# A pooled attention and gMLP kernel: the same instructions issued in another order

## The chip, the cores and the metric

The kernel runs on one core of a Trainium2 chip. The metric is the device time of one execution in microseconds (us). A core has four engines that compute, each with a queue of its own that is worked off in order: TensorE (PE in the profile; its weight loads are listed apart as PEld), VectorE (DVE), ScalarE (ACT) and GpSimd (POOL). SyncE (SP) issues all DMA transfers of this kernel, also in order.

## The reference

```python
# q, k, v: 8 batches x 8 heads x 576 rows x 64
k_p = k.reshape(B, H, 72, 8, D).mean(axis=3)          # pooled by 8
v_p = v.reshape(B, H, 72, 8, D).mean(axis=3)
scores = scale * np.matmul(q, k_p.transpose(0, 1, 3, 2))
attn = softmax(scores)                                 # over the 72 pooled keys
x = np.matmul(attn, v_p)                               # -> 8 x 576 x 512, heads side by side
h = gelu(x @ w_in)                                     # 512 -> 1024
u, v = h[..., :512], h[..., 512:]
v_n = (v - mean(v)) / sqrt(var(v) + 1e-6) * g_ln       # along the 512
v_s = einsum('ts,bsd->btd', w_sg, v_n) + b_sg          # mixes the 576 rows
out = x + (u * v_s) @ w_out
```

All is float32. The kernel reaches that precision on PE by splitting an operand into a high part and a rest (names that end in `hi`/`lo` or `h`/`l`) and adding three products.

## The kernel before, in words

The work on a batch is cut into steps, each a Python generator; one call of `next` records the step's next piece, up to its next `yield`. A step's name is a letter and a number: tile 2 of step H is H2.

- A, B: load k and v, each in two halves (`kvraw`). C: load q of two heads (`qraw`). E: load the last 8 pooled rows of k and v (`left`).
- K: pool k and make the block-diagonal weights `kbd`; for batch 0 the pooling is done by 8 accumulating matmuls with the identity, for the others by a reduction on DVE. K2 reduces `left` into `lp`, transposes it on PE (L317) and writes `kbd`. P: the same for v; for batch 0, P2 leaves the masked v rows in the `left` tile itself.
- Q: transpose q on DVE (L372, `qT`). S: scores of two heads on PE, their maximum on DVE (`nmax`, L389), ten exponentials on ACT (`e`, L406), one over the sum on POOL and DVE (L412 to L417), copies of the last columns on POOL (`el`).
- L and T: transpose `el` and `e` on PE (L126), copy on ACT to `lt` and `ah`. V: attention times v, then `x` and its split `xhl`.
- H: x times the v half of w_in, Gelu (`vg`, L510 to L516), normalisation, split to `vhh`, `vhl`. U: x times the u half, Gelu (`u`, L553). W: row mixing with w_sg, then `u` times it (L567, L569) and the split `ghi`, `glo`. O: times w_out, plus x. Z: transpose on DVE and store.
- In small letters stand the weights, once: `lv`, `lu`, `lo`, `ls` load them, v, u, o convert a chunk of w_in or w_out (ACT L186, DVE L190 to L192, ACT L194 and L195, POOL L197 to L199), s transposes and splits a piece of w_sg (PE L221, ACT L147 or L227, DVE L149).

Two tables of such names set the order. `PROLOGUE` is run once; it holds the weights, batch 0 up to its middle, and the start of batches 1 and 2. `PERIOD` is then run for each batch: `H1+0` is the next piece of H1 of this batch, `T0+1` one of the next batch, `Z1-1` one of the batch before. The order in the table is the order in each engine's queue, because every instruction is tied to the one before it on its engine:

```python
    emit(PROLOGUE, 0)
    for b in range(1, B + 3):
        emit(PERIOD, b)
    assert all(next(x, "done") == "done" for x in going.values())
    last = {}
    for ins in nc.cur_bb.bb.instructions:
        if ins.engine in last:
            tc.add_manual_dep(ins, last[ins.engine], mybir.DependencyInfo(
                mybir.DependencyClass.NoSync, mybir.DependencyReason.DATA), reason="order of issue")
        last[ins.engine] = ins.name
```

All matmuls are recorded by the helper `mm` (L92). PSUM has two rings of two tiles each: `mps` (scores of batch 0, weight chunks of the v half, s, H, U, W, O) and `aps` (scores of the other batches, pooling, T, L, V). A ring's tile can only be written anew when its last reader has gone.

Of the kernel before, what the change touches and what calls it, by code (L numbers as in the profile page):

```python
# [20 lines left out]


PROLOGUE = """
lv0 A1+0 K1+0 A0+0 v0 K1+0 K0+0 C0+0 E0+0 v0 Q0+0 C1+0 K2+0 K0+0 v1 v0 v1 K2+0 lv1 C2+0 K2+0 B0+0 Q1+0 S0+0 S0+0
S1+0 S0+0 S1+0 S0+0 A0+1 S1+0 Q2+0 S2+0 C3+0 S0+0 T0+0 v1 P0+0 v0 v1 S2+0 S1+0 T0+0 Q3+0 B1+0 ls0 S2+0 lu0 S3+0
S3+0 P1+0 S2+0 S3+0 S3+0 lo0 S2+0 v2 S3+0 S1+0 A1+1 C0+1 P2+0 v2 v2 v3 s3 L0+0 T1+0 v3 s3 v2 K0+1 L0+0 V0+0 v3
T1+0 V0+0 lu1 v3 u0 u0 u1 u1 V1+0 V1+0 s3 T2+0 T2+0 T3+0 u0 Q0+1 s1 K1+1 u1 V2+0 C1+1 T3+0 u0 V3+0 u2 u2 V0+0 s1
E0+1 s1 V3+0 s2 V2+0 s4 s2 Q1+1 s4 K2+1 V3+0 K2+1 u1 K2+1 S0+1 V3+0 S1+1 V1+0 V2+0 u2 B1+1 s2 P1+1 u3 S0+1 s4
V0+0 C2+1 V1+0 H1+0 S0+1 H0+0 u3 H1+0 B0+1 u2 s0 P0+1 u3 P2+1 u3 C3+1 S0+1 S0+1 Q3+1 A1+2 S1+1 Q2+1 S2+1 s0 o0
H1+0 H0+0 S1+1 s0 S2+1 H0+0 C0+2 K1+2 S1+1 U2+0 A0+2 S2+1 H1+0 H1+0 U2+0 H3+0 H0+0 o0 H1+0 H0+0 S3+1 V2+0 H4+0  # L30
S2+1 T0+1 Q0+2 o0 H0+0 H3+0 S3+1 H4+0 P2+1 o0 S3+1 H3+0 H2+0 H4+0 H2+0 K0+2 S3+1 H3+0 H4+0 U0+0 S2+1 U3+0 S3+1
U0+0 T0+1 S1+1 H3+0 L0+1 P2+1 H4+0 H2+0 H2+0 U1+0 H3+0 H2+0 T0+1 P2+1 L0+1 T1+1 L0+1 L0+1 U3+0 H4+0 C2+2 H2+0
V0+1 o1 lo1 o1 T1+1 B0+2 H4+0 H4+0 W0+0 E0+2 o1 T1+1 K2+2 o1 V1+1 U1+0 V0+1 o2 W1+0 K2+2 W0+0 o2 V1+1 T2+1 B1+2
W2+0 o2 T2+1 o3 o3 K2+2 o3 T2+1 C1+2 V2+1 o2 W2+0 T3+1 V2+1 W1+0 S0+2 o3 W3+0 S0+2 T3+1 W1+0 W2+0 W2+0 Q1+2 W0+0
W0+0 W1+0 S0+2 T3+1 W3+0 V3+1 O1+0 V3+1 P1+2 W3+0 O0+0 Q2+2 S0+2 P0+2 S1+2 S1+2 W3+0 V1+1 O1+0 C3+2 A1+3 S0+2
O1+0 S2+2 O0+0 V2+1 V0+1 V3+1 P2+2 Z1+0 O2+0 O0+0 C0+3 S1+2 O2+0 S2+2 S1+2 O2+0 Z0+0 Z0+0 H2+1 S2+2 V3+1 T0+2
H2+1 A0+3 V1+1 Q3+2
""".split()
PERIOD = """
H1+0 H1+0 P2+1 U3+0 T0+1 Z1-1 H2+0 H2+0 H2+0 H1+0 C1+2 S2+1 H1+0 P2+1 S3+1 O3-1 H2+0 V2+0 S3+1 O3-1 H1+0 Z2-1  # L40
K1+2 U3+0 H1+0 S1+1 V0+0 S3+1 H3+0 O3-1 K0+2 H3+0 H0+0 H0+0 S3+1 H4+0 S3+1 T0+1 B0+2 H4+0 H3+0 H3+0 H3+0 H0+0
H4+0 S2+1 Q1+2 U2+0 H0+0 H3+0 U1+0 H4+0 Z2-1 H4+0 H0+0 L0+1 U2+0 P2+1 H0+0 H4+0 U0+0 L0+1 L0+1 H4+0 L0+1 V0+1
T1+1 U1+0 Z3-1 H4+0 U0+0 E0+2 W0+0 T1+1 V0+1 T1+1 V1+1 W0+0 Q0+2 V1+1 T2+1 T2+1 W2+0 T2+1 C3+2 W2+0 T3+1 W0+0
V2+1 T3+1 V2+1 T3+1 K2+2 W1+0 B1+2 W2+0 K2+2 W0+0 W1+0 V3+1 V2+1 V1+1 K2+2 W1+0 V3+1 W3+0 P1+2 W1+0 W3+0 Z3-1
W2+0 S0+2 S1+2 O0+0 V3+1 S0+2 O1+0 C2+2 A1+3 S1+2 W3+0 Q2+2 P0+2 W3+0 O0+0 S0+2 S0+2 O1+0 S2+2 V0+1 O0+0 Z0+0
V3+1 S2+2 H2+1 S1+2 V1+1 P2+2 O1+0 Z1+0 Q3+2 S2+2 Z0+0 H2+1 S1+2 O2+0 S0+2 O2+0 T0+2 A0+3 C0+3 O2+0
""".split()


# [619 lines left out]
```

## Time and profile before

| | |
|---|---|
| runs shown | 611.53, 609.78, 611.51 us; median 611.51 |
| the profiled execution's own time | 601.74 us, span 600.0 us |
| mean granted clock of TensorE | 0.975 |
| busy: PE, DVE, ACT, POOL | 93%, 67%, 61%, 40% |
| chain that ended last | PE 83%, ACT 6%, DVE 3%, POOL 3%, DMA 2% |

The profile is that of one further execution; all places below are in microseconds from the start of its span. A row of the timeline has the start, the duration, the engine, the line of the program, the operation, what is written and read, how many instructions are merged into it, and in brackets how long the engine stood idle before it and for whom. A row of the waits has who waited for whom, the total, how often and the longest. A matmul of float32 operands leaves more than one record. The granted clock is 1.00 or 0.50 of TensorE's full rate at any moment.

### The profile page before, as it was taken

The page shows a single profiled execution, that of the slowest core. Times are in us where ns is not written, and L with a number is a line of the kernel's source. Part 1 is how long each engine was busy: PE and PEld are TensorE (multiplying, and loading weights), DVE is VectorE, ACT ScalarE, POOL GpSimd, SP SyncE. Part 2 cuts the span into 40 slices and gives each one's busy share as a digit, 9 for nine tenths or more (in the row PEclk, how much of TensorE's full clock was granted, in tenths as well). Part 3 has the DMA queues.
Part 4 walks back from the last instruction along what each step waited for, and adds up shares of the span by engine and source line. Part 5 has one row for each costly group of instructions (what it writes and reads, how often), then busy time and mean ns, then how long its engine had stood idle before and what let it go on. Part 6 is the DMA issues. An engine that isn't in the chain of part 4 may idle for free.

```text
span 600.0 us, 10376 instructions
## 1 busy us (share of the span) xinstructions
PE 559.0 (93%) x3769; PEld 523.1 (87%) x3769; DVE 401.1 (67%) x532; ACT 363.4 (61%) x1093; POOL 239.6 (40%) x336
## 2 busy tenths in 40 slices
PE   4568589999999999999999999999999999999995
PEld 3454468899899998999899999999899989998995
DVE  2566689778866777587856786677857765434444
ACT  1687599786864775567754974577654885312310
POOL 2276486466333534053425333253315233343230
PEclk9779698999999999999999999999999999999998
DMA  7994624313542253515341334416250210021104
GB/s 195 240 271 103 160 55 126 73 21 74 114 93 37 51 99 66 104 36 100 70 93 28 87 58 92 76 36 116 56 103 11 39 21 14 8 36 25 21 1 79
DMA packets 165954, 46.33 MB, mean 77 GB/s; under 512 B 153424, under 2 KB 153424, under 8 KB 165904
## 3 DMA queue, kind: packets, MB, share of 16 engines
q1 hardware_dynamic: 165904, 45.69, 35.7%
q8 instruction: 29, 0.48, 0.3%
q14 instruction: 21, 0.17, 0.1%
HBM read 36.23 MB, written 9.44 MB: 76 GB/s over the span
## 4 chain that ended last, share of the span: by engine, by line
PE 83%; ACT 6%; DVE 3%; POOL 3%; DMA 2%; SPq 1%; issue 1%; DVEq 0%; ACTq 0%; POOLq 0%
PE mps L92 68%; PE aps L92 12%; PE aps L126 3%; ACT e L406 3%; DMA left<-in_v 1%; SPq L144 1%; DMA raw<-in_moe_w_in 1%; DVE lp L294 1%; POOL wil L199 1%; POOL vg L197 1%; POOL top L198 1%; ACT L406 0%; DVE x L594 0%; PE mps L221 0%; ACT ah L449 0%
## 5 line engine op out<-in xcount | busy, mean ns | idle before, releaser
L578 POOL TENSOR_TENSOR glo<-u,ghi 128x576 fp32r<-128x576 f32 x32 | 45.3, 1429 | 112.7 <-ACT ghi L576 112.7
L92 PE MATMUL mps<-xhl,wih 128*128 128x288 f32 x512 | 89.8, 297 | 0.0
L406 ACT ACTIVATE e<-aps,nmax 128x72 f32<-128x72 f32 x280 | 85.4, 350 | 2.1 <-DVE nmax L389 1.8
L92 PE MATMUL mps<-wih,xhl 128*128 128x512 f32 x256 | 86.2, 403 | 0.1
L92 PEld LDWEIGHTS mps<-xhl,wih 128*128 128x128 f32 x512 | 75.8, 188 | 1.6 <-ACT vg L516 0.2
L406 ACT ACTIVATION_READ_ACCUMULATOR e<-aps,nmax 128x1 f32 x280 | 66.0, 236 | 0.0
L567 DVE SCALAR_TENSOR_TENSOR mps<-mps,gcol,bbc 128x576 f32<-128x576 f32 x32 | 26.4, 825 | 53.0 <-PE mps L92 53.0
L92 PEld LDWEIGHTS mps<-wih,xhl 128*128 128x128 f32 x256 | 48.6, 190 | 10.8 <-DVE x L594 0.3
L92 PE MATMUL mps<-wsh,vhh 128*128 128x288 f32 x256 | 55.9, 300 | 0.0
L92 PE MATMUL mps<-ghi,woh 128*128 128x288 f32 x256 | 55.9, 299 | 0.1
L92 PE MATMUL mps<-xhl,wil 128*128 128x288 f32 x256 | 55.0, 296 | 0.0
L92 PE MATMUL mps<-glo,woh 128*128 128x288 f32 x256 | 54.9, 296 | 0.0
L92 PE MATMUL mps<-wsh,vhl 128*128 128x288 f32 x256 | 54.8, 295 | 0.0
L92 PE MATMUL mps<-wsl,vhh 128*128 128x288 f32 x256 | 54.8, 295 | 0.0
L92 PE MATMUL mps<-ghi,wol 128*128 128x288 f32 x256 | 54.7, 294 | 0.0
L483 POOL TENSOR_TENSOR xhl<-x,xhl 128x576 fp32r<-128x576 f32 x32 | 45.2, 1424 | 23.2 <-ACT xhl L481 23.2
L526 DVE TENSOR_SCALAR vg<-vg,mv,rstd 128x512 f32<-128x512 f32 (+1 forms) x40 | 39.4, 987 | 20.2 <-POOL rstd L524 20.1
L92 PE MATMUL mps<-wil,xhl 128*128 128x512 f32 x128 | 50.8, 397 | 0.0
L516 ACT ACTIVATE vg<-mps 128x512 f32<-128x512 f32 x32 | 19.1, 598 | 46.0 <-PE mps L92 45.8
L536 POOL TENSOR_TENSOR vhl<-vg,vhh 128x512 fp32r<-128x512 f32 x32 | 42.1, 1317 | 9.9 <-ACT vhh L534 9.9
L412 POOL TENSOR_TENSOR ssum<-ssum,eps 128x10 f32<-128x10 f32 x32 | 7.0, 217 | 97.2 <-ACT e L406 97.1
L576 ACT CAST ghi<-u 128x576 fp32r<-128x576 f32 x32 | 21.3, 673 | 37.6 <-DVE u L569 37.6
(137 smaller groups left out, 1431.0 us busy)
## 6 DMA issues: line engine op xcount, KB each, us to landing
qraw<-in_q SPq DMA_DIRECT2D x128, 72.0 KB
out<-y SPq DMA_DIRECT2D x128, 72.0 KB
kvraw<-in_k SPq DMA_DIRECT2D x32, 256.0 KB
kvraw<-in_v SPq DMA_DIRECT2D x32, 256.0 KB
raw<-in_moe_w_in SPq DMA_DIRECT2D x4, 1024.0 KB
raw<-in_moe_w_out SPq DMA_DIRECT2D x2, 1024.0 KB
stage<-in_moe_w_sg SPq DMA_DIRECT2D x4, 288.0 KB
left<-in_k SPq DMA_DIRECT2D x16, 64.0 KB
```

What stands on the lines that cost most here:

```text
L92: nc.tensor.matmul(o, lhsT, rhs, start=start, stop=stop)
L126: nc.tensor.transpose(ps[:rows, i * P:(i + 1) * P], src(i), ident if i < NT - 1 else swap)
L144: nc.sync.dma_start(o, i)
L406: nc.scalar.activation(e[:, i, h], slots[i][:, h], AF.Exp, bias=nmax[:, i, h:h + 1], **acc)
L412: nc.gpsimd.tensor_tensor(ssum, ssum, eps[:, 0:1].unsqueeze(2).broadcast_to([P, NT, 2]), op=ALU.add)
L483: nc.gpsimd.tensor_tensor(xhl[:, 1, g], x32[:, g], xhl[:, 0, g].bitcast(F32), op=ALU.subtract)
L516: nc.scalar.activation(vg, o, AF.Gelu_apprx_tanh)
L526: nc.vector.tensor_scalar(vg, vg, mv[:, 0:1], rstd, op0=ALU.subtract, op1=ALU.mult)
L536: (nc.gpsimd if i < NT - 1 else nc.vector).tensor_tensor(lo, vg, hi.bitcast(F32), op=ALU.subtract)
L567: nc.vector.scalar_tensor_tensor(vs, vs, gcol[:, d:d + 1], bbc.rearrange("p (a n) -> p a n", a=2), op0=ALU.mult, op1=ALU.add)
L576: nc.scalar.copy(ghi[:, d], uf)
L578: nc.gpsimd.tensor_tensor(glo[:, d], uf, ghi[:, d].bitcast(F32), op=ALU.subtract)
```

## The change

The two tables have other contents. No step, tile or instruction is added or taken away, only their order differs, in every queue. The first line of each table:

```diff
 PROLOGUE = """
-lv0 A1+0 K1+0 A0+0 v0 K1+0 K0+0 C0+0 E0+0 v0 Q0+0 C1+0 K2+0 K0+0 v1 v0 v1 K2+0 lv1 C2+0 K2+0 B0+0 Q1+0 S0+0 S0+0
+A0+0 lv0 E0+0 A1+0 v1 K0+0 v0 C1+0 K2+0 v1 K0+0 Q1+0 C0+0 K1+0 K1+0 v0 Q0+0 K2+0 K2+0 v1 S0+0 B0+0 v0 C3+0 v1
...
 PERIOD = """
-H1+0 H1+0 P2+1 U3+0 T0+1 Z1-1 H2+0 H2+0 H2+0 H1+0 C1+2 S2+1 H1+0 P2+1 S3+1 O3-1 H2+0 V2+0 S3+1 O3-1 H1+0 Z2-1
+T0+1 H2+0 H1+0 V2+0 Z2-1 V0+0 H1+0 H2+0 S2+1 H4+0 H2+0 H4+0 U3+0 S3+1 Z1-1 P2+1 H4+0 H1+0 O3-1 O3-1 H4+0 H1+0
```

Three places of the beginning, first as they stood and then as they stand.

SP's queue at the very start. Before:

```order
L144 DMA raw<-in_moe_w_in 128x2x1024
L144 DMA kvraw<-in_k 64x2x512 x4
L144 DMA qraw<-in_q 32x18x32 x4
L144 DMA left<-in_k 32x1x512 x2
L144 DMA left<-in_v 32x1x512 x2
L144 DMA qraw<-in_q 32x18x32 x4
```

And after the change:

```order
L144 DMA kvraw<-in_k 64x2x512 x2
L144 DMA raw<-in_moe_w_in 128x2x1024
L144 DMA left<-in_k 32x1x512 x2
L144 DMA left<-in_v 32x1x512 x2
L144 DMA kvraw<-in_k 64x2x512 x2
L144 DMA qraw<-in_q 32x18x32 x8
L144 DMA kvraw_187<-in_v 64x2x512 x2
```

The first half of k moves to the front, `left` ahead of the second half and of all q tiles.

PE's queue from the first scores of batch 0 to its first V (`ah,vb`), before:

```order
L92 MATMUL mps<-kbd,qT 128x144 x15
L126 MATMUL aps<-ident,e 128x128 x4
L126 MATMUL aps<-swap,e 128x128
L92 MATMUL aps<-kvraw_186,ident 128x128 x8
L92 MATMUL mps<-kbd,qT 128x144 x5
L92 MATMUL aps<-kvraw_186,ident 128x128 x8
L221 MATMUL mps<-ident,stage 128x128 x4
L221 MATMUL mps<-ident,stage 128x64
L126 MATMUL aps<-ident,el 64x128 x4
L126 MATMUL aps<-swap,el 64x128
L126 MATMUL aps<-ident,e 128x128 x4
L126 MATMUL aps<-swap,e 128x128
```

After:

```order
L92 MATMUL mps<-kbd,qT 128x144 x10
L92 MATMUL aps<-kvraw_187,ident 128x128 x8
L92 MATMUL mps<-kbd,qT 128x144 x5
L126 MATMUL aps<-ident,e 128x128 x4
L126 MATMUL aps<-swap,e 128x128
L92 MATMUL mps<-kbd,qT 128x144 x5
L92 MATMUL aps<-kvraw_187,ident 128x128 x8
L126 MATMUL aps<-ident,el 64x128 x4
L126 MATMUL aps<-swap,el 64x128
L126 MATMUL aps<-ident,e 128x128 x4
L126 MATMUL aps<-swap,e 128x128
L221 MATMUL mps<-ident,stage 128x128 x4
```

The first pooling of v (P0, `kvraw` with `ident`) moves ahead of the third scores, and the first transposes of w_sg (`stage`) move behind L0 (`el`) and T1 (`e`).

ACT's queue from the softmax of S0 of batch 1, before:

```order
L406 ACTIVATE e,ssum<-aps,nmax 128x72 x10
L516 ACT_TABLE_LOAD
L516 ACTIVATE vg<-mps 128x512
L194 ACTIVATE raw<-raw 128x4x128
L195 CAST wih<-top 128x4x128
L351 ACTIVATE vbh<-vp 64x4x64 x2
L147 CAST wsh<-mps 128x576
L186 ACTIVATE top<-raw 128x512
L516 ACTIVATE vg<-mps 128x512
L406 ACT_TABLE_LOAD
L406 ACTIVATE e,ssum<-aps,nmax 128x72 x20
L534 CAST vhh<-vg 128x512
```

After:

```order
L406 ACTIVATE e,ssum<-aps,nmax 128x72 x10
L516 ACT_TABLE_LOAD
L516 ACTIVATE vg<-mps 128x512
L351 ACTIVATE vbh<-vp 64x4x64 x2
L516 ACTIVATE vg<-mps 128x512
L406 ACT_TABLE_LOAD
L406 ACTIVATE e,ssum<-aps,nmax 128x72 x10
L147 CAST wsh<-mps 128x576
L406 ACTIVATE e,ssum<-aps,nmax 128x72 x10
L516 ACT_TABLE_LOAD
L516 ACTIVATE vg<-mps 128x512
L534 CAST vhh<-vg 128x512 x2
```

The weight pieces (L194, L195, L186) leave this place, ahead of the softmax or behind it, the w_sg copy (L147) moves between the softmaxes of S1 and S2, and the Gelu of a third H comes at once behind them.

More of the change, by code (lines that the diff above doesn't have):

```diff
@@ L23 @@
 PROLOGUE = """
-lv0 A1+0 K1+0 A0+0 v0 K1+0 K0+0 C0+0 E0+0 v0 Q0+0 C1+0 K2+0 K0+0 v1 v0 v1 K2+0 lv1 C2+0 K2+0 B0+0 Q1+0 S0+0 S0+0
[L25 to L37, printed above, removed]
+A0+0 lv0 E0+0 A1+0 v1 K0+0 v0 C1+0 K2+0 v1 K0+0 Q1+0 C0+0 K1+0 K1+0 v0 Q0+0 K2+0 K2+0 v1 S0+0 B0+0 v0 C3+0 v1
+S0+0 A0+1 S0+0 S1+0 S1+0 P0+0 C2+0 S0+0 Q2+0 S1+0 S1+0 S2+0 Q3+0 v0 T0+0 T0+0 S1+0 lv1 S2+0 S0+0 S2+0 B1+0 S3+0
@@ new lines @@
+S3+0 S3+0 C0+1 P1+0 Q0+1 S2+0 S2+0 ls0 P2+0 v2 lu0 S3+0 v2 S3+0 v2 C1+1 v3 L0+0 v2 T1+0 L0+0 v3 v3 K0+1 s1 V0+0
+v3 lo0 Q1+1 T1+0 V0+0 T2+0 u0 A1+1 V1+0 T2+0 s1 s1 V1+0 T3+0 lu1 s3 V0+0 u1 u0 u1 s3 u0 V2+0 s3 K1+1 T3+0 u1
+V2+0 V3+0 V0+0 V1+0 s2 s2 s2 E0+1 u0 B1+1 K2+1 u2 K2+1 u1 u2 C2+1 V3+0 K2+1 s4 B0+1 u2 u3 P1+1 S0+1 u3 S0+1 V2+0
+V3+0 s4 V1+0 S1+1 u2 s4 H0+0 P0+1 H1+0 Q2+1 u3 S0+1 S1+1 H0+0 S0+1 P2+1 S2+1 s0 H1+0 A1+2 u3 S1+1 C3+1 H1+0 s0
+Q3+1 S2+1 H2+0 H0+0 S2+1 S0+1 C0+2 S1+1 s0 H2+0 H1+0 H1+0 S1+1 P2+1 S3+1 S2+1 H1+0 H0+0 H2+0 H0+0 H0+0 H3+0 U3+0
@@ new lines @@
+V3+0 V2+0 T0+1 lo1 o0 S3+1 H2+0 P2+1 P2+1 H3+0 S2+1 U3+0 H2+0 H2+0 H3+0 H3+0 H4+0 U1+0 C1+2 S3+1 o0 H4+0 S3+1
+H4+0 T0+1 o0 S3+1 T0+1 K1+2 L0+1 A0+2 H3+0 H4+0 U0+0 o0 U1+0 U2+0 L0+1 H3+0 T1+1 H4+0 L0+1 o2 L0+1 U2+0 U0+0
+H4+0 o2 H4+0 B1+2 o1 V0+1 H4+0 T1+1 o1 o1 T1+1 W1+0 V1+1 K0+2 W1+0 o1 V0+1 Q0+2 o3 W0+0 o3 W0+0 T2+1 o2 o3 E0+2
+o2 T2+1 W2+0 V1+1 C2+2 T3+1 T2+1 V2+1 W2+0 o3 K2+2 T3+1 V0+1 T3+1 W0+0 B0+2 W3+0 W0+0 P0+2 W1+0 V2+1 K2+2 W2+0
+W1+0 Q1+2 V3+1 K2+2 W3+0 S0+2 V3+1 S1+2 S0+2 W2+0 W3+0 Q2+2 O0+0 W3+0 V1+1 O0+0 P1+2 V3+1 O0+0 S0+2 O1+0 O1+0
@@ L38 @@
+S1+2 S0+2 S2+2 Z0+0 S2+2 S0+2 A0+3 V1+1 O2+0 S1+2 O1+0 V2+1 S2+2 V3+1 A1+3 O2+0 C0+3 S1+2 P2+2 Z0+0 H2+1 O2+0
+C3+2 T0+2 Z1+0 H2+1 Q3+2
 """.split()
 PERIOD = """
-H1+0 H1+0 P2+1 U3+0 T0+1 Z1-1 H2+0 H2+0 H2+0 H1+0 C1+2 S2+1 H1+0 P2+1 S3+1 O3-1 H2+0 V2+0 S3+1 O3-1 H1+0 Z2-1
-K1+2 U3+0 H1+0 S1+1 V0+0 S3+1 H3+0 O3-1 K0+2 H3+0 H0+0 H0+0 S3+1 H4+0 S3+1 T0+1 B0+2 H4+0 H3+0 H3+0 H3+0 H0+0
-H4+0 S2+1 Q1+2 U2+0 H0+0 H3+0 U1+0 H4+0 Z2-1 H4+0 H0+0 L0+1 U2+0 P2+1 H0+0 H4+0 U0+0 L0+1 L0+1 H4+0 L0+1 V0+1
-T1+1 U1+0 Z3-1 H4+0 U0+0 E0+2 W0+0 T1+1 V0+1 T1+1 V1+1 W0+0 Q0+2 V1+1 T2+1 T2+1 W2+0 T2+1 C3+2 W2+0 T3+1 W0+0
@@ L44 @@
-V2+1 T3+1 V2+1 T3+1 K2+2 W1+0 B1+2 W2+0 K2+2 W0+0 W1+0 V3+1 V2+1 V1+1 K2+2 W1+0 V3+1 W3+0 P1+2 W1+0 W3+0 Z3-1
-W2+0 S0+2 S1+2 O0+0 V3+1 S0+2 O1+0 C2+2 A1+3 S1+2 W3+0 Q2+2 P0+2 W3+0 O0+0 S0+2 S0+2 O1+0 S2+2 V0+1 O0+0 Z0+0
-V3+1 S2+2 H2+1 S1+2 V1+1 P2+2 O1+0 Z1+0 Q3+2 S2+2 Z0+0 H2+1 S1+2 O2+0 S0+2 O2+0 T0+2 A0+3 C0+3 O2+0
+T0+1 H2+0 H1+0 V2+0 Z2-1 V0+0 H1+0 H2+0 S2+1 H4+0 H2+0 H4+0 U3+0 S3+1 Z1-1 P2+1 H4+0 H1+0 O3-1 O3-1 H4+0 H1+0
+S2+1 Z2-1 H4+0 S3+1 P2+1 H1+0 U3+0 H4+0 T0+1 O3-1 H1+0 H2+0 U0+0 S3+1 S3+1 H4+0 U0+0 S1+1 S3+1 H3+0 H3+0 H0+0
@@ new lines @@
+L0+1 P2+1 U2+0 K0+2 H0+0 H3+0 H3+0 H3+0 H0+0 H0+0 U1+0 H0+0 L0+1 Z3-1 U2+0 T1+1 B0+2 H3+0 L0+1 L0+1 H4+0 V0+1
+T1+1 T1+1 Q0+2 H0+0 W0+0 K1+2 T2+1 U1+0 W0+0 E0+2 V0+1 W0+0 V1+1 B1+2 T2+1 K2+2 C2+2 W2+0 V1+1 T2+1 V2+1 C1+2
+T3+1 W2+0 V0+1 W0+0 W2+0 P0+2 T3+1 W1+0 Z3-1 P1+2 V2+1 T3+1 W1+0 V1+1 W1+0 K2+2 W3+0 W2+0 K2+2 W3+0 A0+3 V3+1
+S0+2 V3+1 Q1+2 S0+2 W1+0 V3+1 O0+0 W3+0 S1+2 W3+0 S1+2 A1+3 O1+0 Q2+2 S0+2 S0+2 V1+1 O0+0 S1+2 O1+0 S0+2 O0+0
+S2+2 Z0+0 S2+2 O2+0 O2+0 V2+1 O1+0 Z1+0 P2+2 V3+1 O2+0 C3+2 S2+2 C0+3 H2+1 S1+2 H2+1 Q3+2 Z0+0 T0+2
```

## The prediction

> **What bounds the kernel now.** I read the page first, then the busy time of TensorE (PE) by stretch, the chain that ended last, the waits of PE, and the clock in short windows.
>
> ```profile
> span 600.0 us, 10376 instructions
> ...
> PE 559.0 (93%) x3769; PEld 523.1 (87%) x3769; DVE 401.1 (67%) x532; ACT 363.4 (61%) x1093; POOL 239.6 (40%) x336
> 0.00:132.00 132.00, 97.44 (x563) 0.90 0.56 141
> 132.00:590.00 458.00, 457.62 (x3180) 1.00 0.30 58
> 590.00:600.00 10.00, 3.91 (x30) 0.84 0.60 103
> 155.14 17.04 PE mps L92 x104
> 221.16 17.04 PE mps L92 x104
> ```
>
> The columns of the three stretches, and of those below, are length, busy time of PE (matmul records), granted clock, DMA share and GB/s. From 132 to 590 us PE is idle 458.00 - 457.62 = 0.38 us at full clock, and one batch follows the other after 221.16 - 155.14 = 66.02 us. Matmuls are neither added nor removed, so that part can only get worse. The last 6.09 us (10.00 - 3.91) are the end chain of the last output tile, whose steps keep their order. What an order can win lies ahead of 132 us: 132.00 - 97.44 = 34.56 us of idle PE, and time at half clock.
>
> ```profile
> PE aps L317 <- DVE lp L294: 6.3, 2, 5.2
> PE mps L221 <- DVE top L191: 5.5, 1, 5.5
> PE mps L92 <- DVE qT L372: 5.2, 1, 5.2
> PE mps L92 <- ACT u L553: 2.3, 1, 2.3
> 16.63:20.05 3.42, 2.40 (x19) 1.00 1.09 304
> 20.05:23.46 3.41, 0.45 (x4) 0.99 0.88 222
> 23.50:30.20 6.70, 4.50 (x20) 0.50 1.00 238
> ...
> 37.20:43.80 6.60, 3.60 (x15) 0.50 1.01 287
> 40.53:43.94 3.41, 3.32 (x15) 0.51 0.96 186
> 57.59:61.00 3.41, 1.89 (x12) 1.00 0.14 38
> 61.10:71.10 10.00, 3.94 (x15) 0.50 0.84 187
> 88.28:91.69 3.41, 1.53 (x7) 1.00 0.00 0
> 91.80:95.00 3.20, 3.20 (x12) 0.50 0.61 99
> ```
>
> The clock drops at 23.46, 37.1, 61.0 and 91.7 and returns at 30.3, 43.9, 71.2 and 95.1: always multiples of about 3.41 us apart. So it is set once per tick of 3.41 us, by how busy PE was since the tick before: 0.45, 1.89 or 1.53 us of 3.41 closed it, 2.40 left it open, 3.32 opened it. A hole of 1.5 to 3 us closes the gate or not by where the ticks fall. In the four closed stretches PE was busy 4.50 + 3.60 + 3.94 + 3.20 = 15.24 us, which is 7.6 us more than at full clock.
>
> **Against the Trainium skill.** "TensorE: Matmul & The Clock Gate" says, under the table on why this matters for kernels, to avoid idle gaps of PE over about 3 us. By that the hole of 2.3 us ahead of 90.16 would have cost no clock; the row 88.28:91.69 and the half clock behind it say that it did, so the measurement decides. In its part on the PE-mode transpose the page says that transposes do not count as busy for the gate. That would speak against this change, which puts transposes into holes; but the stretch 40.53:43.94 holds transposes alone, and the clock opened at its end. By that rule the second term of A below would shrink from 1.7 to about 1.
>
> **The change, part by part.** All instructions stay; I follow the new order from hole to hole with the durations of these rows, picked from the timeline and, where no engine's instruction is named in full, from the chain of waits.
>
> ```profile
> 14.38 1.93 DVE L294 TENSOR_REDUCE lp<-left 64x128 f32<-64x1024 f32 x1 [1.50 <-DMA left<-in_v]
> 17.78 2.72 PE L92 MATMUL mps<-kbd,qT 128*128 128x144 f32 x20 [1.02 <-ACT kbd L325]
> 20.25 6.16 ACT e L406 x40
> 24.78 0.77 DVE L372 STREAM_TRANSPOSE qT<-qraw 128x576 f32<-128x576 f32 x1
> 25.70 2.74 PE L92 MATMUL mps<-kbd,qT 128*128 128x144 f32 x10 [5.20 <-DVE qT L372]
> 42.82 1.26 ACT L435 COPY lt<-aps 32x576 f32<-32x576 f32 x2 [0.56 <-PE aps L126]
> 44.14 0.75 PE L92 MATMUL aps<-ah,vb 128*128 128x288 f32 x2 [0.29 <-ACT lt L435]
> 56.78 0.75 PE L92 MATMUL aps<-lt,left 32*128 32x288 f32 x2
> 64.17 1.91 DVE L294 TENSOR_REDUCE lp<-left 64x128 f32<-64x1024 f32 x1 [3.75 <-DMA left<-in_v]
> 67.63 4.45 PE L92 MATMUL aps<-kbd,qT 128*128 128x144 f32 x20 [1.02 <-ACT kbd L325]
> ```
>
> *A, from the start to V0+0 (44.14).* First the loads: ahead of and with `left` stood 1024 (w_in) + 1024 (k) + 288 (q) + 256 KB, landed at 14.38, some 180 KB/us. Now `left` is third in SP's queue, with 1792 KB, and the second k pair and both q tiles follow, 2880 KB in all: landed at about 16 at that pace. The transpose of q (0.77) follows behind a w_in chunk's DVE operations: first scores at about 17.5 (an estimate) instead of 17.78: -0.3, between -1.5 and +1.5, since the q tiles go out later than before. Second, S2+0 (25.70) waits for a transpose of q that stands on DVE (24.78) behind the end of the first softmax, and it still does. But the eight matmuls of P0+0 now stand ahead of it, inside the hole of 5.20; if they run there, the tick after 20.05 sees some 2 us more work, like the stretch 16.63:20.05, and S2+0 takes 1.4 instead of 2.74. ACT is the path from here: two softmaxes take 6.16, and the w_in casts that stood between softmax S1 and S2 stand ahead of S0 now, where ACT waited for scores. Together -1.7 at the end of S3's softmax (-3 if nothing else is late, 0 if ACT has to wait for S2 anyway). Third, the hole of 5.5 (the wait for L191 above): transposes of w_sg waited there for a PSUM tile that a w_in chunk held, and L0+0 and T1+0 were queued behind them. Now these come first and wait only for the softmax; but the copies of lt (42.82) stand on ACT behind the four operations of one chunk and the first of the next, which takes most of that back. I take another 0. Sum of A: -2.0, bounds -4.5 and +1.5.
>
> *B, V0+0 to the last V3+0 matmul (44.14 to 57.53, 13.4).* One buffer ah serves T and V in turn, so each V waits for an ACT copy behind the V before. The new order has T2 and T3 between them, and eight ACT operations stand between the copies for V2 and V3, at 0.63 each (as lt's two in 1.26) 5.0 in all, where V2 itself takes 4 pairs of at most 0.75, under 3. So V3 starts later: +1.2, bounds -0.5 and +2.
>
> *C, the hole of the next batch's `left` (57.53 to 67.63).* Its tile still holds the masked v rows of batch 0, so the load waits for V3+0's last matmul (56.78 + 0.75) in both orders: landing 64.17, reduce, transpose, scores at 67.63. 10.1 us stay. The last w_sg transposes move behind K2+1's; they ran in the hole and still do: 0. Their two ACT copies (1.3) come ahead of S0+1's softmax now.
>
> ```profile
> 70.44 0.91 DVE L389 TENSOR_REDUCE nmax<-aps 128x10 f32<-128x720 f32 x1 [1.73 <-PE aps L92]
> 72.08 5.59 PE mps L92 x24
> 78.81 1.46 PE L92 MATMUL aps<-kbd,qT 128*128 128x144 f32 x10 [0.50 <-DVE qT L372]
> 80.19 1.28 ACT L406 ACT_TABLE_LOAD   x1
> 81.49 5.30 ACT e L406 x35
> 89.46 0.66 ACT u L553
> 90.16 0.50 PE L92 MATMUL mps<-wih,xta 128*128 128x512 f32 x1 [2.28 <-ACT u L553]
> 109.19 0.37 PE L92 MATMUL aps<-ah,vbh 128*128 128x288 f32 x1 [1.32 <-DVE lt L441]
> ```
>
> *D, the first projections with the next batch's scores (67.63 to 109.19, 41.6).* Before, PE waits 0.5, 2.28 and 1.32 here, and the closed clock costs 3.20 / 2 = 1.6. New: S0+1's softmax could start at 71.4 (the maximum at 70.44 plus 0.91); C's two copies and the weight casts on ACT make it about 72.4. Then come its 3.1 (half of 6.16), a table switch (1.28), two Gelu at 0.66 like u's, two casts of v (0.8) and a switch back: S1+1's softmax runs from 80.2 to 83.3, and reciprocal and product (some 1.3) free its PSUM tile at 84.6. PE meanwhile does two H to 77.7 (72.08 + 5.59), S2+1 (1.4), w_sg transposes (0.8) and H2+0 (5.59 / 2 = 2.8): to 82.7; then S3+1 waits 1.9 for that tile. The same list, carried on behind S3+1's softmax and its two switches, gives waits of 0.7, 0.4 and 1.1 ahead of H4, U0 and U2 for PSUM tiles that a Gelu frees. Sum 4.1, as before. If the 1.9 doesn't close the gate the 1.6 are saved, if it does nothing is; I take the middle, -0.8. Bounds -3.5 and +4: here ACT is nearly as full as PE.
>
> *E, the rest.* The V and W part behind 109.19 and the eight batches have the same distance of a whole W tile between a transpose and its V: 0, bounds -0.5 (no idle left to take) and +2.
>
> Sum: -2.0 + 1.2 + 0 - 0.8 + 0 = -1.6 us on the profiled execution, whose own time is 601.74 (span 600.0 and 1.74 around it): 600.1.
>
> **From the profile to the timed runs.** The three runs shown took 609.78 to 611.53, with median 611.51: 9.8 us over the profiled execution of the same instructions. Nothing behind 132 us can be slower on a full PE, so the ahead part differs. Ticks that fall otherwise do that: a resumed PE waits from 3.41 (it starts on a tick) to 6.8 us (just behind one) for the clock, so each closing costs between 1.7 and 3.4, and gaps of 1.3 to 2.3 may close it too. Four closings cost 7.6 in the profile; at worst they cost 4 x 3.4 = 13.6, and two more by small holes up to 6.8. So the timed runs look like an unlucky tick. In the new order the first of the long holes is broken up and one of 2.28 becomes pieces; I count one closing less, at the unlucky price and the middle of 1.7 and 3.4: -2.6, besides A's share. 611.5 - 1.6 - 2.6 = 607.3.
>
> **Rivals.**
> 1. *No change that can be told.* The four long holes close the gate as before, since the largest (C) stays and P0+0's loads may land too late to fill the first. Then only the sum counts: 611.5 - 1.6 = 609.9. For it speaks that C is 10.1 of the 34.56; against it, that at least the hole ahead of S2+0 has work to fill it.
> 2. *Timed runs as good as the profile.* The new order has no hole that an unlucky tick makes long, and runs like before's own profiled execution: 600 to 602. For it speaks that those instructions did run in 601.74; against it that C remains and must close the gate.
> 3. *Slower, by ACT in D.* If S1+1's softmax starts as late as before (81.49 instead of the 80.2 of my list), S3+1 waits 3.2 instead of 1.9, which closes the gate wherever the tick falls; two ticks to open instead of one cost 3.4 instead of 1.6. D is then 1.3 + 1.8 = +3.1. Without the closing saved that is 611.5 - 2.0 + 1.2 + 3.1 = 613.8, and 615.8 if A gives nothing. It decides as soon as that wait passes 3 us. For it speaks that the chain of waits runs over ACT alone from the switch at 80.19 to 90.16; against it, that H's Gelu come earlier.
>
> **How the numbers follow.** Two kernels differ visibly here when they are over 0.3% (1.8 us) apart. Forecast (605 to 609.6): 0.41; rival 2 and what lies between: 0.16; rival 1: 0.20; rival 3: 0.16; a later start by the q loads (A at +1.5, B at +2): 0.07. So faster 0.57, same 0.20, slower 0.23. The range reaches from rival 2's upper half, 601, to rival 3's lower, 614.5, and leaves out about 2 in 10. For the forecast alone it is 604 to 610.
>
> **What would show it.** In the changed profile: first scores near 17.5; P0+0's matmuls between S1+0 and S2+0 and the clock at 1.0 there; no wait of w_sg transposes (L221) for L191; V3+0 ending near 57; the `left` wait still 5 us or more; a wait of S3+1 for DVE or ACT near 84; a period of 66.0. A period over 66.1, or PE idle of more than 1 us between 132 and 590 us, would make me wrong in E; a wait over 3 us near 84 makes rival 3 right; a median at 610 with fewer closings in the profile makes the gate the wrong reason for the 9.8 us.

## The result, and the profile after

| | runs | median us | lowest to highest |
|---|---|---|---|
| before | 20 | 611.08 | 601.62 to 615.08 |
| changed | 20 | 615.34 | 611.31 to 623.69 |

The ratio is 1.0132, with a 95% interval of 1.0091 to 1.0173; the forecast was 607.3, on the other side. The ratio leaves out every run that is over 1.5% above the fastest of its kernel, which here drops part of a spread that belongs to the kernel (below), so medians of all runs stand beside it: 615.34 / 611.08 = 1.0070, +4.3 us. The median of the changed kernel lies at the edge of a gap (its eleventh run in order of time took 615.50, the twelfth 620.34), so the means are given too: 610.50 and 617.37, +6.9 us. By each of the three it is slower. Both kernels run in groups: of before's 20 runs four lie at 601.6 to 608.0 and sixteen at 609.7 to 615.1; of the changed kernel's eleven at 611.3 to 615.5 and nine at 620.3 to 623.7. The groups go with the granted clock, which was 0.968 to 0.982 in the changed kernel's lower group and 0.949 to 0.957 in its upper one.

The page and the stretches of the changed kernel (own time 612.89 us, a time of the lower group), with the columns of the prediction:

```profile
span 610.0 us, 10388 instructions
PE 560.4 (92%) x3769; PEld 524.2 (86%) x3769; DVE 409.9 (67%) x532; ACT 362.5 (59%) x1093; POOL 241.4 (40%) x336
0.00:132.00 132.00, 97.12 (x555) 0.91 0.55 139
132.00:600.00 468.00, 459.36 (x3188) 1.00 0.29 58
158.29 11.99 PE mps L92 x72
225.73 11.99 PE mps L92 x72
```

The page counts 12 instructions more than before's, but the engines' own counts are the same. Up to 132 us the sums hardly changed: 97.12 us of PE work instead of 97.44, at a clock of 0.91 instead of 0.90. The loss is where before had no idle PE: from 132 to 600 us PE is idle 468.00 - 459.36 = 8.64 us, where it was 0.38 (up to 590 us), and a batch takes 225.73 - 158.29 = 67.44 us, where it took 66.02. The first of the waits of PE names the reason:

```profile
PE aps L92 <- DVE lt L441: 8.5, 6, 1.4
PE aps L126 <- POOL el L423: 8.1, 2, 5.8
PE aps L317 <- DVE lp L294: 5.3, 1, 5.3
```

A wait of 1.4 us for `lt`, six times, once for each batch that follows. The timeline of one of these places, with ACT's, DVE's and PE's rows by start:

```profile
237.54 0.60 PE L126 MATMUL aps<-ident,el 128*64 128x128 f32 x4
241.81 0.62 ACT L534 CAST vhh<-vg 128x512 fp32r<-128x512 f32 x1 [2.91 <-DVE vg L526]
242.34 0.62 ACT L438 CAST lt<-aps 32x576 fp32r<-32x576 f32 x1
243.63 0.65 ACT L553 ACTIVATE u<-mps 128x576 f32<-128x576 f32 x1
244.49 0.60 PE L126 MATMUL aps<-ident,e 128*128 128x128 f32 x4
245.06 0.63 ACT L439 CAST lt<-aps 32x576 fp32r<-32x576 f32 x1
245.72 0.75 DVE L441 TENSOR_TENSOR lt<-aps,lt 32x576 fp32r<-32x576 f32 x1 [1.34 <-ACT lt L439]
246.62 0.38 PE L92 MATMUL aps<-ah,vbh 128*128 128x288 f32 x1 [1.42 <-DVE lt L441]
```

L0's transposes (`ident,el`) are done by 238.3. Their copy (L438) needs nothing else, but in ACT's queue it stands behind the cast of H0 (L534), which waits 2.91 us for a normalisation on DVE; so it starts at 242.34. A second delay is Gelu of U (L553) between the two halves. `aps` has two tiles: T1 (`ident,e`) has taken the other one, so V0 can only have L0's, and that is released by the last reader, L441 at 245.72 + 0.75. The order before:

```profile
234.89 0.62 ACT L534 CAST vhh<-vg 128x512 fp32r<-128x512 f32 x1 [1.04 <-DVE vg L526]
238.03 0.60 PE L126 MATMUL aps<-ident,el 128*64 128x128 f32 x4
238.78 0.63 ACT L438 CAST lt<-aps 32x576 fp32r<-32x576 f32 x1 [2.59 <-PE aps L126]
241.76 0.30 PE L92 MATMUL aps<-ah,vbh 128*128 128x288 f32 x1
```

There the cast came ahead of L0, ACT was waiting for the transposes, and V0 went before T1 and took the other tile. The normalisation itself (L526) is slower after the change, 1128 ns in the mean instead of 987; but it is as slow (1125) in e3 below, where the wait is gone. So the 1.4 us per batch come from the place of L0's copies in the queue.

### The profile page after: what moved, and what is told of

Read it like the earlier page. It is cut to its first block, busy times and chain, and to the rows that moved or that the text cites. A ratio compares the mean times of both kernels' runs of the same rounds, so it can differ in the third digit from the quotient of the medians.

```text
span 610.0 us, 10388 instructions
## 1 busy us (share of the span) xinstructions
PE 560.4 (92%) x3769; PEld 524.2 (86%) x3769; DVE 409.9 (67%) x532; ACT 362.5 (59%) x1093; POOL 241.4 (40%) x336
## 4 chain that ended last, share of the span: by engine, by line
PE 75%; ACT 9%; DVE 8%; issue 3%; DMA 2%; POOL 2%; SPq 1%; DVEq 0%; ACTq 0%; POOLq 0%
PE mps L92 61%; PE aps L92 11%; ACT e L406 4%; PE aps L126 3%; DVE vg L526 1%; DVE lt L441 1%; ACT lt L439 1%; DMA left<-in_v 1%; ACT lt L438 1%; SPq L144 1%; DVE top L191 1%; ACT vg L516 1%; ACT vhh L534 1%; DVE bst L520 1%; POOL rstd L524 1%
## 5 line engine op out<-in xcount | busy, mean ns | idle before, releaser
L526 DVE TENSOR_SCALAR vg<-vg,mv,rstd 128x512 f32<-128x512 f32 (+1 forms) x40 | 45.1, 1128 | 24.9 <-POOL rstd L524 24.7
L92 PE MATMUL mps<-ghi,woh 128*128 128x288 f32 x256 | 57.3, 305 | 0.1
L523 POOL TENSOR_TENSOR rstd<-mv,eps 128x1 f32<-128x1 f32 (+1 forms) x40 | 7.5, 188 | 107.8 <-DVE mv L521 107.8
```

Of the source, the lines that this page charges most:

```text
L92: nc.tensor.matmul(o, lhsT, rhs, start=start, stop=stop)
L523: nc.gpsimd.tensor_tensor(rstd, mv[:, 1:2], eps[:n, 1:2], op=ALU.add)
L526: nc.vector.tensor_scalar(vg, vg, mv[:, 0:1], rstd, op0=ALU.subtract, op1=ALU.mult)
```

## The experiments

Two tables and two suspects (the period's `lt`, and the clock) make a small grid. First the tables apart.

```diff
 # e1 against the changed kernel: the PERIOD of before (first line alone shown)
-T0+1 H2+0 H1+0 V2+0 Z2-1 V0+0 H1+0 H2+0 S2+1 H4+0 H2+0 H4+0 U3+0 S3+1 Z1-1 P2+1 H4+0 H1+0 O3-1 O3-1 H4+0 H1+0
+H1+0 H1+0 P2+1 U3+0 T0+1 Z1-1 H2+0 H2+0 H2+0 H1+0 C1+2 S2+1 H1+0 P2+1 S3+1 O3-1 H2+0 V2+0 S3+1 O3-1 H1+0 Z2-1
 # e2 against the changed kernel: the PROLOGUE of before (first line alone shown)
-A0+0 lv0 E0+0 A1+0 v1 K0+0 v0 C1+0 K2+0 v1 K0+0 Q1+0 C0+0 K1+0 K1+0 v0 Q0+0 K2+0 K2+0 v1 S0+0 B0+0 v0 C3+0 v1
+lv0 A1+0 K1+0 A0+0 v0 K1+0 K0+0 C0+0 E0+0 v0 Q0+0 C1+0 K2+0 K0+0 v1 v0 v1 K2+0 lv1 C2+0 K2+0 B0+0 Q1+0 S0+0 S0+0
```

> New PROLOGUE table, old PERIOD table. Theory P (the new period makes PE wait 1.42 us for lt ahead of V0 of each batch): no such wait, 66.0 us from batch to batch, a span near 601 (600.0 plus the 1.5 that the new beginning is longer by), ratio to before 0.998 to 1.006. Rival Q (the beginning and its closed clock cost the time): a period of 66.0 as well, but a span near 608 and a ratio of about 1.013.

> Old PROLOGUE table, new PERIOD table. Theory P: the wait of about 1.4 us for lt ahead of V0 in each batch, 67.4 us from batch to batch, a span near 608 to 610 and a ratio of 1.011 to 1.016. Rival Q: the wait may be there, but the ratio is 1.000 to 1.004.

Before took 611.64 in the median on that chip (30 runs, one of them 934.9 at a granted clock of 0.56), e1 613.2 (601.1 to 615.6, 12 runs) and e2 618.69 (611.5 to 623.3, 12 runs). e1 lies where before does, with no wait for `lt` and a period of 66.03, though its profile has a span of 610.5 where 601 was expected; the reason follows below. e2 has the loss and its wait among PE's:

```profile
PE aps L92 <- DVE lt L441: 10.2, 7, 1.7
```

So the loss is in the new period. Whether that wait makes it was tried by moving three pieces of L0 in it, and nothing else (e3 against the changed kernel, one stretch of the table):

```diff
-L0+1 P2+1 U2+0 K0+2 H0+0 H3+0 H3+0 H3+0 H0+0 H0+0 U1+0 H0+0 L0+1 Z3-1 U2+0 T1+1 B0+2 H3+0 L0+1 L0+1 H4+0 V0+1
+L0+1 P2+1 U2+0 K0+2 H0+0 L0+1 H3+0 H3+0 H3+0 H0+0 L0+1 H0+0 U1+0 L0+1 H0+0 Z3-1 U2+0 T1+1 B0+2 H3+0 H4+0 V0+1
```

> The changed kernel, with three pieces of step L0+1 (the copies and subtractions that make lt) moved in PERIOD ahead of the cast of H0 and of its normalisation. Theory P: PE no longer waits for lt, 66.0 us from batch to batch, span 600 to 602, ratio 0.998 to 1.006. Rival Q: ratio stays at 1.010 to 1.015. A third way, that ACT or DVE is simply late there: the wait turns to another one of about 1 us (ah, al or a PSUM tile), period 67.

e3 took 607.48 (601.9 to 614.8; only six runs, so the median is rough). Its row of the copy, now directly behind the Gelu, and its period, 225.09 - 159.31 = 65.78:

```profile
237.65 0.62 ACT L438 CAST lt<-aps 32x576 fp32r<-32x576 f32 x1
159.31 11.98 PE mps L92 x72
225.09 11.98 PE mps L92 x72
```

Counted from the row of 72 matmuls the copy starts 237.65 - 225.09 = 12.56 us after it, where it was 242.34 - 225.73 = 16.61 in the changed kernel; no wait for `lt` is left among PE's, and the period is even 0.24 us under that of before. T1 still goes ahead of V0 here, so that alone costs nothing when the copies are early. This settles the loss of 1.4 us a batch. It does not explain why identical programs spread over 14 us. Both kernels were run once more, with no edit:

> The changed kernel once more, for the clock of each run: its runs fell in two groups, near 613 and near 622. Theory G (the gate): the wait of 1.4 us in each batch closes the clock for a tick when the ticks fall badly; a run near 622 has a mean clock near 0.95, one near 613 near 0.975, and if the profile is of the upper group it shows half clock behind the waits for lt between 150 and 530 us. Rival: the two groups have the same clock, and something else (transfers) is slower.

> The kernel before once more, for a profile of one of its usual times. Theory V: TensorE's clock is closed by the hole of 5 us ahead of the first V of batch 0; if no tick opens it before V starts, it stays closed through all of V of batch 0 (13.4 us become some 25), and the run takes 608 to 615; the profile then shows one closed stretch of over 30 us from about 38 on and the same 66.0 us per batch. If the run takes 601 to 605, the closed stretch ends before V0+0 as in the first profile. Rival D (transfers): a slow run has the same closed stretches and late landings of kvraw, qraw or raw instead.

The changed kernel came out the same (615.25, 609.5 to 622.9 in 12 runs), again in two groups, the lower with a clock of 0.968 to 0.984, the upper with 0.957 to 0.959. Its profile is of the lower group, so where the clock of the upper one is closed was not seen. The one run of before took 608.95, with a span of 607.2 instead of 600.0, and the profile shows where: its clock stayed closed from 41.8 to 58.9 (17 us, not the over 30 that were expected), through the first half of the matmuls of V of batch 0, where the first profile of before has full clock. The most extreme case among the profiles is e1's (span 610.5). Ticks of 3.41 us in it, with PE's busy time and the granted clock, and two rows of its timeline:

```profile
38.96:42.38 3.42, 2.52 (x12) 0.50 0.96 313
59.44:62.86 3.42, 3.42 (x6) 0.50 0.02 5
76.51:79.92 3.41, 3.41 (x15) 0.50 0.39 121
79.92:83.34 3.42, 3.42 (x21) 1.00 0.63 161
43.28 1.33 PE L92 MATMUL aps<-ah,vb 128*128 128x288 f32 x2
44.54 1.32 PE L92 MATMUL aps<-lt,left 32*128 32x288 f32 x2
```

From 42.4 to 66.3, in seven ticks, PE is recorded busy without a break (V, and some transposes between), and the clock stays at 0.50, though 3.32 us opened it in the prediction's row 40.53:43.94. It comes back behind a tick of transposes and scores (76.51). In e7 it came back earlier, inside V, behind the tick 55.48 to 58.90, of which 2.6 us are transposes. What is special here is V of batch 0: half of its matmuls have weights of 32 rows (`lt,left`, 32*128). Two ways to try it: keep the clock open ahead of V, or change V.

```diff
 # e5: ten more matmuls of 288 columns behind the last pooling of v, into an unused half of its PSUM tile
+                if i == 1 and b in BY_PE:
+                    for _ in range(WARM):
+                        mm(st["warm"][:, 1, 0:HALF], ident, raw[:, 0, 0:HALF], True, True)
...
 # e9: the 128-row product of V twice; the product of the last 8 pooled keys is left out
-                mm(o, vl[:, g // 2, gl:gl + 2], lt[64:96, sl], False, True)
+                mm(o, vb[b][:, g], ah[:, sl], False, True)
...
 # e4: the masked v rows of batch 0 in a tile of their own, so that `left` comes free earlier
+        if b in WHOLE:
+            v32 = per.tile([96, 2, 4, D], F32, name="vl")[64:96]
```

> The old order with ten more matmuls of 288 columns with the identity behind P1+0, into an unused bank, where PE stood idle for 5.5 us (it adds work, the result is not used). Theory V: the clock stays open or opens before V of batch 0, nearly all runs take 600 to 605, median 1 to 1.6% under before. Rival D: no change, median 610 to 613. If ten matmuls delay L0+0: 1 to 2 us more in all runs.

> The old order; V of batch 0 leaves out the product of the last 8 keys (weights of 32 rows) and runs the one of 128 rows a second time in its place, so the count and size of matmuls are the same. Theory V32 (matmuls that use 32 of 128 rows don't count enough to open the clock): the clock opens within two ticks inside V, and the upper group near 611 to 615 moves to 602 to 606. Rival V4 (all float32 matmuls of this length don't open it at half clock): two groups as before, median 610 to 613.

> The old order; the masked v rows of batch 0 go to the tile vl instead of staying in left, so that the next batch's left can load before V3+0. Term C of the prediction (10.1 us between V3+0 and S0+1): the wait for lp shrinks from 5.2 us to under 2, S0+1 starts about 5 us earlier behind V3+0, and the first H is then bound by xhl; 2 to 5 us less in runs of the same kind, with the spread of the runs unchanged (two groups some 10 us apart). Rival: xhl and the weight chunks on POOL hold the first H at the same time, no gain.

Before took 611.85 in the median here. e5 took 609.34 (605.2 to 613.3, and one run of 642.1), where 600 to 605 was expected: no clear gain. Its profile says why keeping warm failed. The clock was open when V began and closed inside V:

```profile
45.81:49.23 3.42, 2.77 (x8) 0.97 0.71 189
49.23:52.64 3.41, 3.41 (x7) 0.50 0.93 231
```

A tick with 2.77 us of V closed it, where 2.40 us of other matmuls had left it open (the prediction's row 16.63:20.05). e9 took 602.43 (599.8 to 603.4, 4 runs), narrow and 9.4 us below. e4 took 605.81 (599.6 to 609.8), 6.0 below, with a spread of 10 us left: PE's longest wait for `lp` fell from 5.2 to 2.1. But e9 frees `left` early as e4 does, so its gain is not the rows' alone. The version that touches the rows alone is e10: 96 rows for the second product, of which 64 have zero weights.

```diff
+    lt0 = [per.tile([96, S], F32, name="lt", tag=f"lt{gp}") for gp in range(2)]
+    for gp in range(2):
+        nc.gpsimd.memset(lt0[gp][0:64], 1.0)
...
+        if b in WHOLE:
+            nc.gpsimd.memset(t[0:64, :, 0:4 * D], 0.0)       # t is `left`
...
-                mm(o, vl[:, g // 2, gl:gl + 2], lt[64:96, sl], False, True)
+                mm(o, vl[:, g // 2, gl:gl + 2], lt[:, sl], False, True)
```

e11 is e10 with the v rows in a tile of their own, e12 the same with the order of e3, and e6 is e12 without the 96 rows:

```diff
+    v96 = per.tile([96, 2, 4, D], F32, name="vl")            # e11, e12
+    nc.gpsimd.memset(v96[0:64], 0.0)
...
+        if b in WHOLE:
+            v32 = v96[64:96]
```

> The order of the kernel before. For batch 0 alone, the second product of V (the last 8 pooled keys) takes 96 rows instead of 32: rows 0 to 63 of its weights are zero, the rows of lt beside them are one, so the output stays the reference's. Theory (weights of 32 rows don't hold or open the clock): the groups of runs at 610 to 612 and 613 to 615 vanish, median 602 to 605, ratio to before 0.985 to 0.99, and in the profile the clock is back at the latest two ticks behind the start of V. Rival (what counts is other data than zeros, or e9 was quick only because left came free earlier): two groups as before, median 608 to 612, ratio 0.997 to 1.003.

> The 96 rows of e10, and the masked v rows of batch 0 in a tile of their own, so that left of batch 1 needn't wait for the end of V. Theory: both gains together, as in e9 (602.4) or a little below, for e4's lucky runs took 599.6: median 599 to 603, ratio 0.98 to 0.987, no run over 605. Rival: if the zeros don't count, the two groups of e4 stay, 600 to 610, median 605 to 607.

> The changed order with the lt pieces moved ahead in the period (e3), the 96 rows of e10 and left free. Theory: e3's profile had period 65.78 instead of 66.02, six times 0.24 is 1.4, and its clock should no longer depend on where the ticks fall: median 598 to 603, ratio 0.977 to 0.986. Rival: the new beginning has other closings ahead of V (e3: 17 us closed ahead of 43), which 96 rows don't touch, so it stays at 603 to 607.

> e12 without the 96 rows: the changed order with the lt pieces ahead and left free. Theory: the runs fall in two groups as in e3 (602 and 615) and e4 (600 and 610), median 601 to 608, with at least one run 5 us above the fastest. Rival: one narrow group as in e12, which would mean that the new beginning meets no unlucky tick and that the rows don't matter there.

Before took 612.20 on that chip. e10: 604.39 (602.4 to 606.2, 9 runs), ratio 0.990 (0.9864 to 0.9936); e11: 601.46 (600.2 to 602.6, 5 runs), ratio 0.9851 (0.9804 to 0.9898); e12: 602.44 (600.7 to 603.2, 5 runs), ratio 0.9859 (0.981 to 0.9907); e6: 601.0, 602.1, 602.2 and 608.6. The upper groups are gone with 96 rows and still there without (in e6 one run of four). Rows of zero weights serve as well as the full rows of e9 (e11 601.46, e9 602.43), so it isn't the data. e11 shows the opening directly: V begins at 46.72 at half clock, the tick from 47.00 holds 96-row V and nothing else, and at its end the clock is back. e6's profile is of the run of 608.6; its tick from 45.03, of 32-row V, is just as full and the clock stays, until 75.75.

```profile
47.00:50.41 3.41, 3.41 (x8) 0.50 1.01 331
50.41:53.82 3.41, 3.05 (x15) 0.97 0.52 103
47.84 1.17 PE L92 MATMUL aps<-lt,vl 96*128 96x288 f32 x2
51.29 0.65 PE L92 MATMUL aps<-lt,vl 96*128 96x288 f32 x2
51.78 0.65 PE L92 MATMUL aps<-ah,vb 128*128 128x288 f32 x2
45.03:48.44 3.41, 3.41 (x6) 0.50 1.06 348
```

(The first five rows are e11's, the last is e6's.) e11 and e12 beat both kernels. The period of e3 is 0.24 us shorter than before's, 1.4 us in six turns, and still e12 is not ahead of e11 in the median of five runs each; why is open.

With the luck of the clock taken out, the two tables could be weighed again: e13 is the changed kernel with the 96 rows of e10, e14 is e1 with them.

> The changed kernel as it is, with the 96 rows of e10 alone. Theory (the order's own cost is the period's 1.42 us, six times, and what is over 616 us in its runs is the clock closed through V): the group at 620 to 624 vanishes, and the time is e10's 604.4 + 8.5 = 612.9 plus or minus the difference of the beginnings, 609 to 615. Rival (the upper group has another cause than V): runs over 618 remain.

> The new beginning with the old period (e1) and the 96 rows: the beginning's own worth, with the luck of the clock taken out, against e10's 604.4. The prediction's A, B and D alone would give 604.4 - 1.6 = 602.8. Theory: the gains and losses of the beginning cancel, 602 to 606. Rival: the new beginning is the slower one by itself (its three holes for el, for the second half of k and for S3 of batch 1 close the clock once more): over 606.

e13 took 611.96 (609.7 to 613.5, 12 runs), e14 603.49 (602.9 to 606.9, 12 runs), before 611.48 in that comparison. The group over 620 has vanished from the changed order too, and with the wait still there; so the waits for `lt` do not make that group, as had been supposed ahead of e8. e13 still has the wait, e14 has the period of before (222.33 - 156.26 = 66.07):

```profile
PE aps L92 <- DVE lt L447: 8.6, 6, 1.4
156.26 17.05 PE mps L92 x104
222.33 17.05 PE mps L92 x104
```

## Why the prediction was wrong

The kernels at 96 rows against those as they are, by medians, and by means of all runs in the last column:

| | forecast | by medians | by means |
|---|---|---|---|
| the beginning (A, B, C, D) | -1.6 | e14 - e10: 603.49 - 604.39 = -0.9 | 604.05 - 604.33 = -0.3 |
| the period (E) | 0 | e13 - e14: 611.96 - 603.49 = +8.5 | 611.84 - 604.05 = +7.8 |
| timed runs less the luck of the clock | -2.6 | before 611.48 - 604.39 = 7.1; changed 615.34 - 611.96 = 3.4; so -3.7 | 610.50 - 604.33 = 6.2; 617.37 - 611.84 = 5.5; so -0.6 |
| sum | -4.2 | +3.9, against 615.34 - 611.08 = +4.3 | +6.9, as 617.37 - 610.50 |

The medians come from several chips (before itself gave 611.08 to 612.20 on them), so each entry is good to about 1 us at best. The entries add up to the whole by the way that they are formed, so the sum is no check on them. The period's entry is about the same both ways. That of the beginning can't be told from 0, and the third depends on how runs in groups are summed up; it also holds what the 96-row products save at full clock (last section).

**E is the step that failed.** "The same distance of a whole W tile between a transpose and its V" was the reason for a cost of 0. It looked at T and V only. L0, whose tile V0 has to have, was left out, as was the queue in which its copy stands: behind a cast that waits for DVE. The upper bound of +2 would hold one such place; E's cost comes once in each of six periods, 6 x 1.42 = 8.5. An item that repeats needs the count in its bound too. The prediction named the mark of it ("PE idle of more than 1 us between 132 and 590 us"), and did not give it a rival or a chance. That rival 3's times (613.8 and 615.8) enclose the measured 615.34 is luck: its loss was to come in D, and came in E.

The beginning, by its steps:

```profile
19.20 0.77 DVE L372 STREAM_TRANSPOSE qT<-qraw 128x576 f32<-128x576 f32 x1
20.12 4.36 PE L92 MATMUL mps<-kbd,qT 128*128 128x144 f32 x20 [1.47 <-DVE qT L372]
24.32 1.95 PE L92 MATMUL aps<-kvraw,ident 128*128 128x128 f32 x16
28.66 1.46 PE L92 MATMUL mps<-kbd,qT 128*128 128x144 f32 x10 [2.40 <-DVE qT L372]
40.70 1.06 PE L126 MATMUL aps<-ident,el 128*64 128x128 f32 x4 [5.77 <-POOL el L423]
57.28 0.75 PE L92 MATMUL aps<-lt,left 32*128 32x288 f32 x2
66.23 0.47 PE L317 MATMUL aps<-ident,lp 128*128 128x128 f32 x1 [5.26 <-DVE lp L294]
86.45 1.46 PE L92 MATMUL aps<-kbd,qT 128*128 128x144 f32 x10 [2.12 <-DVE e L417]
102.52 0.94 PE L126 MATMUL aps<-ident,el 128*64 128x128 f32 x4 [2.29 <-POOL el L423]
```

- *A, first scores:* 20.12 instead of the forecast 17.5, outside its bounds. The transpose of q that they need is the second one, behind the three operations of a second w_in chunk on DVE, not of one: it starts at 19.20.
- *A, the hole ahead of S2:* right. Pooling of v (24.32) runs in it, S2 takes 1.46 instead of 2.74, and the clock is open there (the tick 24.09:27.51, below), though it was closed for the tick before, which the forecast did not have. S2 still waits 2.40 for its transpose of q.
- *A, the hole of 5.5:* right that the wait for L191 goes and that nothing is gained. The first L now waits 5.77 for `el`, and V of batch 0 starts at 44.13, where it was 44.14: of A's -2.0 nothing came.
- *B:* the last V ends at 57.28 + 0.75 = 58.0, forecast near 57, before 57.5: A gave nothing, so the end of V is 0.5 later instead of 0.8 earlier.
- *C:* the wait stays, 5.26.
- *D:* S3 of batch 1 waits 2.12, where the forecast had 1.9, and it does not close the clock here, so rival 3 fell. But a wait that the list did not have, 2.29 us of L0+1 for `el` at 102.52, closes it 11 us later than before for one tick. In the second profile of the same kernel (e8) both waits close it: that of S3, 2.15 there, falls into the tick 82.80 to 86.21 with 1.26 us of work, and the clock is closed up to 89.6. So which end of D holds, the 1.6 saved or nothing, depends on the tick, and the middle, -0.8, describes neither.

The clock in the changed profile, around three of its four closed stretches:

```profile
20.68:24.09 3.41, 3.41 (x17) 0.51 0.89 213
24.09:27.51 3.42, 2.17 (x19) 0.99 1.06 280
37.75:41.16 3.41, 0.46 (x3) 0.51 0.93 307
41.16:44.57 3.41, 3.41 (x15) 0.50 0.89 142
44.57:47.99 3.42, 3.37 (x14) 0.99 1.06 357
99.18:102.60 3.42, 1.13 (x9) 1.00 0.00 0
102.60:106.01 3.41, 3.41 (x16) 0.51 0.02 5
```

**The 9.8 us between the profile and the timed runs.** The prediction said "an unlucky tick", and was right in that; its price list (1.7 to 3.4 us for each closing) was not the reason. In both profiles on which the forecast and the result rest, the tick from about 41 is filled by transposes ahead of V, but for a first pair of V in the second, and the clock opens behind it (the prediction's 40.53:43.94 with 3.32 us busy, and 41.16:44.57 above with 3.41). In e7 the tick from 41.83 to 45.24 has 2.97 us of such work, in e1 that from 38.96 has 2.52, and the clock stays closed. Then V begins at half clock and its own ticks don't open it; the closed stretch is 17 us in e7 and 41 in e1, and two matmuls of V take 44.54 - 43.28 = 1.26 us in it, where they take 0.68 at full clock (last section). The profile on which the prediction rested (601.74) was as fast as the fastest of before's 20 runs (601.62), so it could not show this. If the upper groups are that case (the 96 rows, which remove them, speak for it; no profile of the changed kernel's upper group was taken), the changed order is in it less often: nine of 20 runs, against sixteen of before's. By the medians that made up for 3.7 of the 8.5 us, by the means for hardly any. The forecast's closing "fewer" is not what the profile shows: it has four, as before.

The Trainium skill says in "TensorE: Matmul & The Clock Gate", in its part on the PE-mode transpose, that transposes do not count as busy for the gate in the same way as other work. The trace does not agree: the tick 41.16:44.57 again is transposes but for the first pair of V, and the clock opens behind it.

## What to carry to other kernels

Where an order of issue is changed in a loop, follow every reader of a ring tile to its place in its own engine's queue, and multiply the bound of any wait by the number of turns; a copy that depends on little is cheap only if nothing ahead of it waits. When runs of one program spread in groups, find out which group the profile belongs to before making the sum against it, look in several profiles for a stretch whose clock differs, and give the mean beside a median that falls near a gap.

## What was not expected of the hardware

- V with 32-row weights did not open a closed clock in seven full ticks (e1), nor hold an open one with 2.77 us of a tick (e5); it did hold one in a fuller tick (before's from 54.18 to 57.59, with 3.30 us). With 96 rows one tick of V opened it (e11). These runs change the number of rows and the row at which they start together, so the two are not told apart.
- The 32-row products are dearer at full clock too: in before two V matmuls start 53.88 - 53.20 = 0.68 us after the two ahead of them (rows below), in e11 51.78 - 51.29 = 0.49. That is part of e10's gain: with the clock open throughout, V takes 12.1 us in e10's profile (46.93 to 59.01) and 13.4 in before's. It may be the gate's reason as well, if PE stands still between matmuls of unlike rows and the records hide it. No run here separates these.

```profile
53.20 0.75 PE L92 MATMUL aps<-ah,vb 128*128 128x288 f32 x2
53.88 0.75 PE L92 MATMUL aps<-lt,left 32*128 32x288 f32 x2
```
